# A decode attention kernel on one core: larger K/V chunks, an output summed in PSUM, and a last step of V that is multiplied turned

## The chip, the cores and the metric

The kernel runs on one core of a Trainium2 chip. The metric is device time in microseconds (us) of that core. "Before" is the kernel as it was, "after" is the changed kernel. A profile of one execution goes with every run; its span is about 2 us shorter than the time. All runs quoted here are of state fast. Times in the profiles are us from the start of the span. The engines are PE (TensorE), DVE (VectorE), ACT (ScalarE), POOL (GpSimd) and SP (SyncE, which here only issues DMAs).

## The reference

One token of 448 features attends to a cache of 65,536 positions, and the result is mixed with a small token MLP by a gate:

```python
B, Sq, D = 1, 1, 448
Hq, Hkv, Sk, Dh = 16, 8, 65536, 256
q = x @ wq                                 # 16 heads, two per K/V head
scores = einsum("bhqd,bhkd->bhqk", q, k) * Dh ** -0.5
o = einsum("bhqk,bhkd->bhqd", softmax(scores), v)
a = o.reshape(B, Sq, Hq * Dh) @ wo
b = ...                                    # layernorm, gelu MLP over F = 1792
g = sigmoid((x * gate_w).sum(-1, keepdims=True))
return g * a + (1 - g) * b                 # 448 numbers
```

All inputs are bf16. K and V together are 537 MB; they are read once. Everything else is small.

## The kernel before

A K/V head is cut in chunks, a chunk in steps of 16 blocks of 128 positions. K and V chunks take turns in a ring of four buffers. For every step, VectorE transposes K (L346), and TensorE multiplies it with the queries (L354). When a chunk's scores are complete, ScalarE takes the exponentials, VectorE transposes those, and TensorE multiplies them with V ("P.V", L376). At the end of a head, the sums are scaled, turned from rows into columns by an fp32 product, and projected with wo.

```python
SB = 16
SIZES = (4,) * 8          # steps per chunk: 4 steps are 32 KB per partition
RING = 4
# ... (cut)
    def load(item):       # items alternate: K of chunk i, V of chunk i
        last = sizes[-1]
        if item < 2 * total - 2:
            piece(item, 0, sizes[item // 2 % n_chunks] * SB)      # one DMA per chunk
        elif item == 2 * total - 1:                                # last chunk: 1 MB pieces
            for s in range(last - 1):
                piece(item - 1, s * SB, SB)                        # K 0, 1, 2
            piece(item, 0, SB)                                     # V 0
            piece(item - 1, (last - 1) * SB, SB)                   # K 3
            for s in range(1, last - 1):
                piece(item, s * SB, SB)                            # V 1, 2
            tail = SB // 2 - 2
            piece(item, (last - 1) * SB, SB - tail)
            piece(item, last * SB - tail, tail)
# ... (cut)
    for i in range(total):
        g, c = divmod(i, n_chunks)
        for s in range(sizes[c]):
            turn(i, s, n)          # VectorE: transpose K into kT[n % 2]
            scores(i, s, n)        # TensorE: 8 matmuls into sc[i % 2]
            # ... (cut: MLP, previous head's output)
        if 2 * i + RING < 2 * total:
            load(2 * i + RING)
        softmax(i)                 # ScalarE exp, VectorE transpose
        if c == n_chunks - 1:
            den_sum(g)
            den_tot(g)
        for s in range(sizes[c]):
            p_v(i, s)              # TensorE: 8 matmuls of 4 rows each (last step cut: in two parts)
        if 2 * i + 1 + RING < 2 * total:
            load(2 * i + 1 + RING)
        if c == n_chunks - 1:
            o_scale(g)             # VectorE: pvs = pv / denominator
    o_turn(HKV - 1)                # TensorE, fp32: rows to columns
    o_out(HKV - 1)                 # TensorE: @ wo; VectorE: + acc
    nc.sync.dma_start(out=out[0, 0].rearrange("(o n) -> o n", o=1), in_=res[:])
```

The softmax here doesn't subtract the row's maximum and nothing guards it: scores larger than these inputs give would overflow.

## Time and profile before

| | before |
|---|---|
| time, median of 3 | 1277.08 us (1277.07 to 1277.14) |
| span of the profile | 1275.1 us |
| busy: PE, DVE | 59%, 52% |
| DMA | 544.88 MB, 427 GB/s over the span |

The first fence is from the page: the busy share of the 16 DMA engines in 40 equal slices of the span, in tenths, and what they moved.

```profile
DMA  9999999999999999999999999999999999999996
GB/s 393 434 431 430 436 432 427 436 433 430 435 430 430 433 434 432 432 434 428 433 435 427 435 433 430 432 434 430 431 435 431 430 433 435 430 433 435 428 433 276
```

DMA is full from the second slice to the last but one. Only the beginning and the last slice (32 us) leave room, and in the last slice compute still has to finish what arrived last. The second fence is the timeline of before in that slice: start, duration, engine, line, operation, operands; in brackets the idle time of the engine before it and who ended it.

```profile
1239.05 2.31 DVE L346 STREAM_TRANSPOSE kT_183<-ring_70 128x2048 f32<-128x2048 f32 x1 [5.98 <-DMA ring_70<-in_A_k_cache_dram]
...
1257.28 2.27 DVE L346 STREAM_TRANSPOSE kT_183<-ring_72 128x2048 f32<-128x2048 f32 x1
1260.91 2.31 DVE L346 STREAM_TRANSPOSE kT_184<-ring_72 128x2048 f32<-128x2048 f32 x1 [1.36 <-DMA ring_72<-in_A_k_cache_dram]
1263.28 1.89 PE L354 MATMUL sc_75<-kT_184,qw 128*128 128x512 bf16 x8 [1.78 <-DVE kT_184 L346]
1265.21 0.60 ACT L361 ACTIVATE p_186<-sc_75 128x512 bf16<-128x512 f32 x1 [12.98 <-PE sc_75 L354]
...
1267.05 2.04 PE L376 MATMUL pv_77<-ring_73,pT_188 128*4 128x512 bf16 x32
...
1269.14 0.75 DVE L393 TENSOR_SCALAR pvs<-pv_77,rden 128x512 f32<-128x512 f32 x1 [1.61 <-PE pv_77 L376]
1269.94 1.05 PE L402 MATMUL misc<-sel,pvs 128*128 128x2 f32 x8 [0.85 <-DVE pvs L393]
...
1271.25 0.92 PE L412 MATMUL misc<-wo_97,oT 128*1 128x448 bf16 x4 [0.25 <-DVE oT L406]
1272.20 0.61 DVE L417 TENSOR_TENSOR res<-acc,misc 1x448 bf16<-1x448 f32 x1 [1.01 <-PE misc L412]
1272.84 0.32 SPq L452 DMA_DIRECT2D out_dram<-res  x1
```

Read it from the bottom. The store is issued at 1272.84. Before it stand, one after the other, the addition, the projection, the fp32 turn, the scaling and P.V. Further up, VectorE waited 1.36 us for the last piece of K (1260.91). What the timeline does not print is when the last piece of V landed. The trace's semaphore records give it: 1268.66, the last of the 16 increments that report this load (in what follows that time is its landing). The last weights load of P.V came at 1268.71, so the last K and the last V arrive at P.V together.

The trace's DMA records also give the time of single K/V packets (one row of a buffer is one packet):

```
before: packet bytes, count, median ns
 8192     896    309
32768   16128   1213
```

### The profile page before, as it was taken

The page shows a single profiled execution, that of the slowest core. Times are in us where ns is not written, and L with a number is a line of the kernel's source. Part 1 is how long each engine was busy: PE and PEld are TensorE (multiplying, and loading weights), DVE is VectorE, ACT ScalarE, POOL GpSimd, SP SyncE. Part 2 cuts the span into 40 slices and gives each one's busy share as a digit, 9 for nine tenths or more (in the row PEclk, how much of TensorE's full clock was granted, in tenths as well). Part 3 has the DMA queues.
Part 4 walks back from the last instruction along what each step waited for, and adds up shares of the span by engine and source line. Part 5 has one row for each costly group of instructions (what it writes and reads, how often), then busy time and mean ns, then how long its engine had stood idle before and what let it go on. Part 6 is the DMA issues. An engine that isn't in the chain of part 4 may idle for free.

```text
span 1275.1 us, 10091 instructions
## 1 busy us (share of the span) xinstructions
PE 758.4 (59%) x4374; PEld 288.1 (23%) x4374; DVE 661.7 (52%) x429; ACT 62.7 (5%) x159; POOL 83.1 (7%) x118
## 2 busy tenths in 40 slices
PE   3564656655566556656557565575655655656656
PEld 2121222212222222222122122221222222222212
DVE  7364455554464644646445455464453644545545
ACT  0000000000000000000000000000000000000000
POOL 3111012110021100210000000000000000000000
PEclk9888888888889887898888888788887888879789
DMA  9999999999999999999999999999999999999996
GB/s 393 434 431 430 436 432 427 436 433 430 435 430 430 433 434 432 432 434 428 433 435 427 435 433 430 432 434 430 431 435 431 430 433 435 430 433 435 428 433 276
DMA packets 21154, 544.88 MB, mean 427 GB/s; under 512 B 2675, under 2 KB 2806, under 8 KB 3958
## 3 DMA queue, kind: packets, MB, share of 16 engines
q1 hardware_dynamic: 19730, 540.55, 98.5%
q0 software_dynamic: 1376, 3.69, 0.8%
q8 instruction: 34, 0.56, 0.2%
q14 instruction: 10, 0.08, 0.0%
q10 hardware_dynamic: 4, 0.00, 0.0%
HBM read 544.22 MB, written 0.00 MB: 427 GB/s over the span
## 4 chain that ended last, share of the span: by engine, by line
DMA 64%; DVE 17%; PE 17%; issue 2%; DVEq 0%; SPq 0%; ACT 0%; ACTq 0%
DMA ring_70<-in_A_k_cache_dram 58%; PE sc_74 L354 14%; DVE kT_183 L346 9%; DVE kT_184 L346 7%; DMA ring_72<-in_A_k_cache_dram 6%; PE sc_75 L354 1%; PE misc L402 1%; DVE acc L337 1%; PE misc L412 1%; PE misc L325 0%; DVE acc L417 0%; PE pv_77 L376 0%; DVE pT_188 L365 0%; DVE oT L406 0%; DVEq L346 0%
## 5 line engine op out<-in xcount | busy, mean ns | idle before, releaser
L354 PEld LDWEIGHTS <-qw 128*128 128x128 bf16 x2048 | 222.3, 111 | 772.5 <-issue 324.5
L354 PE MATMUL sc_74<-kT_183,qw 128*128 128x512 bf16 x512 | 190.8, 536 | 239.6 <-DVE kT_183 L346 239.6
L346 DVE STREAM_TRANSPOSE kT_183<-ring_70 128x2048 f32<-128x2048 f32 x64 | 147.6, 2306 | 166.6 <-DMA ring_70<-in_A_k_cache_dram 146.7
L354 PE MATMUL sc_75<-kT_183,qw 128*128 128x512 bf16 x512 | 145.7, 433 | 114.7 <-DVE kT_183 L346 114.7
L346 DVE STREAM_TRANSPOSE kT_183<-ring_72 128x2048 f32<-128x2048 f32 x64 | 147.0, 2297 | 114.3 <-DMA ring_72<-in_A_k_cache_dram 91.7
L354 PE MATMUL sc_74<-kT_184,qw 128*128 128x512 bf16 x512 | 150.9, 445 | 25.4 <-DVE kT_184 L346 25.4
L346 DVE STREAM_TRANSPOSE kT_184<-ring_72 128x2048 f32<-128x2048 f32 x64 | 145.7, 2277 | 4.9 <-PE sc_75 L354 3.4
L346 DVE STREAM_TRANSPOSE kT_184<-ring_70 128x2048 f32<-128x2048 f32 x64 | 145.6, 2275 | 2.8 <-PE sc_74 L354 2.7
L354 PE MATMUL sc_75<-kT_184,qw 128*128 128x512 bf16 x512 | 131.7, 401 | 18.1 <-DVE kT_184 L346 18.1
L365 DVE STREAM_TRANSPOSE pT_187<-p_185 128x512 bf16<-128x512 bf16 x32 | 22.8, 712 | 103.4 <-ACT p_185 L361 103.4
L365 DVE STREAM_TRANSPOSE pT_188<-p_186 128x512 bf16<-128x512 bf16 x32 | 22.8, 712 | 86.7 <-ACT p_186 L361 86.7
L361 ACT ACTIVATE p_185<-sc_74 128x512 bf16<-128x512 f32 x32 | 19.1, 597 | 713.4 <-PE sc_74 L354 713.4
L376 PE MATMUL pv_77<-ring_71,pT_187 128*4 128x512 bf16 x512 | 30.4, 379 | 24.4 <-DVE pT_187 L365 24.4
L376 PE MATMUL pv_76<-ring_71,pT_187 128*4 128x512 bf16 x512 | 30.4, 379 | 24.4 <-DVE pT_187 L365 24.4
L376 PEld LDWEIGHTS <-pT_187 128*4 128x4 bf16 x1024 | 22.1, 86 | 87.3 <-DVE pT_187 L365 64.6
L376 PE MATMUL pv_77<-ring_73,pT_188 128*4 128x512 bf16 x512 | 30.6, 379 | 18.3 <-DVE pT_188 L365 18.3
L376 PE MATMUL pv_76<-ring_73,pT_188 128*4 128x512 bf16 x512 | 30.4, 379 | 18.3 <-DVE pT_188 L365 18.3
L361 ACT ACTIVATE p_186<-sc_75 128x512 bf16<-128x512 f32 x32 | 19.1, 597 | 449.5 <-PE sc_75 L354 449.5
L376 PEld LDWEIGHTS <-pT_188 128*4 128x4 bf16 x1024 | 22.1, 86 | 71.5 <-DVE pT_188 L365 48.4
L337 DVE SCALAR_TENSOR_TENSOR acc<-misc,half_g,acc 1x448 f32<-1x448 f32 x14 | 9.4, 672 | 53.1 <-PE misc L325 53.1
L314 POOL TENSOR_SCALAR t_b<-t_b 128x448 f32<-128x448 f32 x14 | 7.9, 567 | 361.3 <-ACT t_b L306 361.3
L139 POOL DMA_DIRECT2D wo_97<-in_A_wo_dram x4 | 3.1, 784 | 295.4 <-PE misc L412 295.4
(90 smaller groups left out, 201.9 us busy)
## 6 DMA issues: line engine op xcount, KB each, us to landing
ring_70<-in_A_k_cache_dram SPq DMA_DIRECT2D x32, 4096.0 KB, 26.5
ring_71<-in_A_v_cache_dram SPq DMA_DIRECT2D x32, 4096.0 KB, 29.8
ring_72<-in_A_k_cache_dram SPq DMA_DIRECT2D x31, 4096.0 KB, 29.4
ring_73<-in_A_v_cache_dram SPq DMA_DIRECT2D x31, 4096.0 KB, 33.9
ring_72<-in_A_k_cache_dram SPq DMA_DIRECT2D x4, 1024.0 KB, 27.5
ring_73<-in_A_wq_dram SPq DMA_DIRECT2D x1, 3072.0 KB, 10.4
ring_73<-in_A_v_cache_dram SPq DMA_DIRECT2D x3, 1024.0 KB, 26.9
wo_96<-in_A_wo_dram POOLq DMA_DIRECT2D x4, 448.0 KB, 15.1
```

What stands on the lines that cost most here:

```text
L139: nc.gpsimd.dma_start(out=wo_t[g % 2][:], in_=A_wo[g * 512:(g + 1) * 512, :].rearrange("(q p) n -> p q n", p=128),)
L314: nc.gpsimd.tensor_scalar(out=t_b[:], in0=t_b[:], scalar1=GELU_C1, scalar2=1.0, op0=ALU.mult, op1=ALU.add)
L337: nc.vector.scalar_tensor_tensor(out=acc[:], in0=misc[0:1, 0:D], scalar=half_g[0:1, 0:1], in1=acc[:], op0=ALU.mult, op1=ALU.add,)
L346: nc.vector.transpose(out=kT[n % 2][:].bitcast(FP32), in_=kn[:, s * SB * 128:(s + 1) * SB * 128])
L354: nc.tensor.matmul(sc[i % 2][:], lhsT=qw[:, g, q, PAD - s:PAD - s + 128], rhs=kv[:, :, q // 2, :, q % 2], start=(s == 0 and q == 0), stop= ...
L361: nc.scalar.activation(out=p_t[i % 2][:], in_=sc[i % 2][:], func=ACT.Exp, scale=scale, accum_out=den[g % 2][:, c:c + 1],)
L365: nc.vector.transpose(out=pT_t[i % 2][:], in_=p_t[i % 2][:])
L376: nc.tensor.matmul(pv[g % 2][32 * a:32 * a + 4, :], lhsT=pT[:, k, :, s], rhs=vt[:, j * DH:(j + 2) * DH], start=first and k < 4, stop=last ...
L402: nc.tensor.matmul(o_ps[:, 2 * c:2 * c + 2], lhsT=pvs[:, lo:lo + 128], rhs=sel[:, 2 * half:2 * half + 2], start=(half == 0), stop=(half == 1),
L412: nc.tensor.matmul(a_ps, lhsT=oT[:, 2 * c + r:2 * c + r + 1], rhs=wo_t[g % 2][:, 2 * r + c, :], start=(c == 0 and r == 0), stop=(c == 1 an ...
```

## The change

The change has three intents: fewer and larger packets (chunks of 5 or 4 steps, so 40 or 32 KB per partition), less work for VectorE (the output is summed in PSUM by TensorE, the queries are prepared one head at a time), and a shorter tail. For the tail, all pieces of the last K go ahead of V, and the last step of V is multiplied turned: V is the stationary operand, so its product comes out as columns and is added to the turned sum of the earlier steps, which can be turned before the last piece of V has landed. The core of the diff:

```diff
-SIZES = (4,) * 8
+SIZES = (5, 5, 5, 5, 4, 4, 4)
+TAIL = 4
 # load(), last chunk
-            for s in range(last - 1):
-                piece(item - 1, s * SB, SB)
-            piece(item, 0, SB)
-            piece(item - 1, (last - 1) * SB, SB)
-            for s in range(1, last - 1):
-                piece(item, s * SB, SB)
-            tail = SB // 2 - 2
-            piece(item, (last - 1) * SB, SB - tail)
-            piece(item, last * SB - tail, tail)
+            for s in range(last):
+                piece(item - 1, s * SB, SB)
+            for s in range(last - 1):
+                piece(item, s * SB, SB)
+            piece(item, (last - 1) * SB, SB - TAIL)
+            piece(item, last * SB - TAIL, TAIL)
 # ... (cut: denominators per chunk size, queries per head, MLP summed in PSUM)
+    def to_acc(col, rows, stop=False):          # 448 outputs as 4 groups of 112 columns
+        for a in range(4):
+            nc.tensor.matmul(acc[32 * a:32 * a + 1, 0:DQ], lhsT=col,
+                rhs=rows[:, DQ * a:DQ * (a + 1)], ..., tile_position=(0, 32 * a))
+    def p_v_turned(i, s, lo, hi):
+        for j in range(lo, hi):
+            for c in range(2):
+                at = (s * SB + j) * DH + c * 128
+                nc.tensor.matmul(o_ps[:, 2 * c:2 * c + 2], lhsT=vt[:, at:at + 128],
+                    rhs=pT[:, j, :, s], start=False, ...)
 # after the loop
-    o_turn(HKV - 1)
-    o_out(HKV - 1)
-    nc.sync.dma_start(out=out[0, 0].rearrange("(o n) -> o n", o=1), in_=res[:])
+    nc.vector.tensor_copy(out=pvs[:, 0:DH], in_=pv[g % 2][:, 0:DH])
+    nc.scalar.activation(out=pvs[:, DH:2 * DH], in_=pv[g % 2][:, DH:2 * DH], func=ACT.Copy)
+    o_turn(g)
+    p_v_turned(i, s, 0, SB - TAIL)
+    p_v_turned(i, s, SB - TAIL, SB)
+    nc.vector.tensor_tensor(out=oT..., in0=o_ps..., in1=rden..., op=ALU.mult)
+    o_out(g)
+    nc.vector.tensor_scalar(out=res[0:97, :], in0=acc[0:97, 0:DQ], scalar1=bias[0:97, 0:1], ...)
+    nc.sync.dma_start(out=out[0, 0].rearrange("(a n) -> a n", a=4), in_=res[0:97:32, :])
```

More of the change, by code (lines that the diff above doesn't have):

```diff
@@ L57 @@
     DR = D - DA
-    assert DR == 64 and F % 128 == 0 and SK % (128 * SB * sum(SIZES)) == 0
+    DQ = D // 4
+    assert DR == 64 and D % 4 == 0 and F % 128 == 0 and SK % (128 * SB * sum(SIZES)) == 0
     sizes = SIZES * (SK // (128 * SB * sum(SIZES)))
@@ L78 @@
     misc = psum.tile([128, 512], FP32, name="misc")
+    den_ps = psum.tile([128, 512], FP32, name="den_ps")
+    acc = psum.tile([128, 512], FP32, name="acc")
     total = HKV * n_chunks
@@ L132 @@
     nc.gpsimd.dma_start(out=w2T[:], in_=B_w2[:, 0].rearrange("(p b) -> p b", b=NF))
-    b2 = const.tile([1, 1], FP32)
-    nc.gpsimd.dma_start(out=b2[:], in_=B_b2.rearrange("(o n) -> o n", o=1))
+    zb = const.tile([1, 2], FP32)
+    nc.gpsimd.dma_start(out=zb[:, 1:2], in_=B_b2.rearrange("(o n) -> o n", o=1))
     wo_t = [const.tile([128, 4, D], BF16, name=f"wo{i}") for i in range(2)]
@@ L150 @@
     sel = const.tile([128, 4], FP32)
-    pick = const.tile([128, 2], FP32)
-    same = const.tile([128, 64, 2], FP32)
+    classes = sorted(set(sizes), reverse=True)
+    assert list(sizes) == sorted(sizes, reverse=True)
+    pick = const.tile([128, 2, len(classes)], FP32)
     nc.gpsimd.memset(sel[:], 0.0)
     nc.gpsimd.memset(pick[:], 0.0)
-    rows = [(sel, 4, -1, 32 * a) for a in range(4)]
-    rows += [(pick, 2, -16, 32 * a + s) for a in range(4) for s in range(MAXS)]
+    rows = [(sel[:], 4, -1, 32 * a) for a in range(4)]
+    for k, size in enumerate(classes):
+        rows += [(pick[:, :, k], 2, -16, 32 * a + s) for a in range(4) for s in range(size)]
     for t, w, step, row in rows:
         nc.gpsimd.affine_select(
-            out=t[:], in_=t[:], compare_op=ALU.not_equal, fill=1.0, base=-row,
+            out=t, in_=t, compare_op=ALU.not_equal, fill=1.0, base=-row,
             pattern=[[step, w]], channel_multiplier=1,
@@ L165 @@
         nc.gpsimd.memset(block[32 * a:32 * a + 32, a:a + 1], 1.0)
-    nc.gpsimd.tensor_copy(
-        out=same[:], in_=pick[:].rearrange("p (o r) -> p o r", o=1).to_broadcast([128, 64, 2])
-    )
     mhalf = const.tile([128, 1], FP32)
@@ L183 @@
     den = [work.tile([128, n_chunks], FP32, name=f"den{i}") for i in range(2)]
-    dsum = work.tile([128, 1], FP32, name="dsum")
-    rden = work.tile([128, 1], FP32, name="rden")
+    dsum = work.tile([128, len(classes)], FP32, name="dsum")
+    rden = work.tile([128, 2], FP32, name="rden")
     pvs = work.tile([128, 512], FP32, name="pvs")
     oT = work.tile([128, 4], BF16, name="oT")
-    acc = work.tile([1, D], FP32, name="acc")
-    half_g = work.tile([1, 1], FP32, name="half_g")
-    res = work.tile([1, D], BF16, name="res")
+    half_g = work.tile([128, 1], FP32, name="half_g")
+    bias = work.tile([128, 1], FP32, name="bias")
+    res = work.tile([128, DQ], BF16, name="res")
     qT = const.tile([128, 2, HQ], BF16)
-    qw = const.tile([128, HKV, 8, WIN], BF16)
+    qr = const.tile([128, 8, HQ], BF16)
+    qw = [const.tile([128, 8, WIN], BF16, name=f"qw{i}") for i in range(2)]
     gate = const.tile([128, 2], FP32)
-    nc.vector.memset(qw[:], 0.0)
-    for t in pv:
+    for t in pv + qw:
         nc.vector.memset(t[:], 0.0)
-    nc.vector.memset(acc[:], 0.0)
+    nc.vector.memset(acc[:, 0:DQ], 0.0)
     xd = const.tile([1, 2, 128], BF16)
@@ L221 @@
     nc.vector.tensor_tensor(out=xg, in0=x_row[:], in1=gw_row[:], op=ALU.mult)
-    z1 = const.tile([1, 1], FP32)
-    nc.vector.tensor_reduce(out=z1[:], in_=xg, axis=AXIS.X, op=ALU.add)
-    z_ps = misc[:, 500:501]
-    nc.tensor.matmul(z_ps, lhsT=one_f[:], rhs=z1[:], start=True, stop=True)
-    nc.scalar.activation(out=gate[:, 0:1], in_=z_ps, func=ACT.Exp, scale=-1.0)
-    nc.scalar.activation(out=gate[:, 1:2], in_=z_ps, func=ACT.Exp, scale=1.0)
+    nc.vector.tensor_reduce(out=zb[:, 0:1], in_=xg, axis=AXIS.X, op=ALU.add)
+    z_ps = misc[:, 500:502]
+    nc.tensor.matmul(z_ps, lhsT=one_f[:], rhs=zb[:], start=True, stop=True)
+    nc.scalar.activation(out=gate[:, 0:1], in_=z_ps[:, 0:1], func=ACT.Exp, scale=-1.0)
+    nc.scalar.activation(out=gate[:, 1:2], in_=z_ps[:, 0:1], func=ACT.Exp, scale=1.0)
     nc.vector.tensor_scalar(out=gate[:], in0=gate[:], scalar1=1.0, scalar2=None, op0=ALU.add)
     nc.vector.reciprocal(out=gate[:], in_=gate[:])
+    nc.vector.tensor_scalar(
+        out=half_g[:], in0=gate[:, 1:2], scalar1=0.5, scalar2=None, op0=ALU.mult
+    )
+    nc.vector.tensor_tensor(out=bias[:], in0=z_ps[:, 1:2], in1=gate[:, 1:2], op=ALU.mult)
     xb_ps = sc[0][:, 0:D]
@@ L281, with queries @@
             )
-    for g in range(HKV):
+    nc.vector.tensor_copy(out=qr[:].rearrange("p b h -> p (b h)"), in_=qr_ps)
+    def queries(g):
         for r in range(2):
@@ L286 @@
             nc.vector.tensor_tensor(
-                out=qw[:, g, :, cols],
-                in0=qr_ps.rearrange("p (b h) -> p b h", h=HQ)[:, :, h:h + 1].to_broadcast([128, 8, 4]),
+                out=qw[g % 2][:, :, cols], in0=qr[:, :, h:h + 1].to_broadcast([128, 8, 4]),
                 in1=block[:].rearrange("p (o a) -> p o a", o=1).to_broadcast([128, 8, 4]),
@@ L291 @@
             )
+    queries(0)
     load(RING - 1)
@@ L299 @@
     MIX = min(8, (n_steps - 4) // (NF + 1))
+    opened = set()
+    def to_acc(col, rows, stop=False):
+        for a in range(4):
+            nc.tensor.matmul(
+                acc[32 * a:32 * a + 1, 0:DQ], lhsT=col, rhs=rows[:, DQ * a:DQ * (a + 1)],
+                start=a not in opened, stop=stop, tile_position=(0, 32 * a),
+            )
+            opened.add(a)
     def mixer(n):
@@ L320, in mixer @@
             nc.gpsimd.tensor_scalar(
-                out=t_b[:], in0=t_b[:], scalar1=1.0, scalar2=None, op0=ALU.add
+                out=t_b[:], in0=t_b[:], scalar1=1.0, scalar2=half_g[:, 0:1], op0=ALU.add,
+                op1=ALU.mult,
             )
@@ L324, in mixer @@
         if ph == 5:
-            nc.tensor.matmul(
-                misc[0:1, 0:D], lhsT=w2T[:, b:b + 1], rhs=gel[:], start=True, stop=True
-            )
-            if b == 0:
-                nc.vector.tensor_scalar(
-                    out=half_g[:], in0=gate[0:1, 1:2], scalar1=0.5, scalar2=None, op0=ALU.mult
-                )
-                nc.vector.tensor_scalar(
-                    out=acc[:], in0=acc[:], scalar1=b2[0:1, 0:1], scalar2=gate[0:1, 1:2],
-                    op0=ALU.add, op1=ALU.mult,
-                )
-            nc.vector.scalar_tensor_tensor(
-                out=acc[:], in0=misc[0:1, 0:D], scalar=half_g[0:1, 0:1], in1=acc[:],
-                op0=ALU.mult, op1=ALU.add,
-            )
+            to_acc(w2T[:, b:b + 1], gel[:])
     def turn(i, s, n):
@@ L354, in scores @@
             nc.tensor.matmul(
-                sc[i % 2][:], lhsT=qw[:, g, q, PAD - s:PAD - s + 128], rhs=kv[:, :, q // 2, :, q % 2],
+                sc[i % 2][:], lhsT=qw[g % 2][:, q, PAD - s:PAD - s + 128], rhs=kv[:, :, q // 2, :, q % 2],
                 start=(s == 0 and q == 0), stop=(s == sizes[c] - 1 and q == 7),
@@ L365, in softmax, with p_v @@
         nc.vector.transpose(out=pT_t[i % 2][:], in_=p_t[i % 2][:])
-    def p_v(i, s, lo=0, hi=SB // 2):
+    def p_v(i, s):
         g, c = divmod(i, n_chunks)
@@ L371, in p_v @@
         first = c == 0 and s == 0
-        last = c == n_chunks - 1 and s == sizes[c] - 1
-        for k in range(lo, hi):
+        last = (g, c, s) == (HKV - 1, n_chunks - 1, sizes[c] - 2)
+        last |= g < HKV - 1 and c == n_chunks - 1 and s == sizes[c] - 1
+        for k in range(SB // 2):
             j = s * SB + 2 * k
@@ L381, in den_sum @@
     def den_sum(g):
-        nc.vector.tensor_reduce(out=dsum[:], in_=den[g % 2][:], axis=AXIS.X, op=ALU.add)
-    def den_tot(g):
-        d_ps = misc[:, 501:502]
-        nc.tensor.matmul(
-            d_ps, lhsT=same[:].rearrange("p o r -> p (o r)"), rhs=dsum[:], start=True, stop=True
-        )
-        nc.vector.reciprocal(out=rden[:], in_=d_ps)
-        nc.vector.tensor_tensor(out=rden[:], in0=rden[:], in1=gate[:, 0:1], op=ALU.mult)
-    def o_scale(g):
-        nc.vector.tensor_scalar(
-            out=pvs[:], in0=pv[g % 2][:], scalar1=rden[:, 0:1], scalar2=None, op0=ALU.mult
-        )
+        for k, size in enumerate(classes):
+            lo = sizes.index(size)
+            nc.vector.tensor_reduce(
+                out=dsum[:, k:k + 1], in_=den[g % 2][:, lo:lo + sizes.count(size)], axis=AXIS.X,
+                op=ALU.add,
+            )
+    def den_tot(g):
+        for k in range(len(classes)):
+            nc.tensor.matmul(
+                den_ps[:, 0:2], lhsT=dsum[:, k:k + 1].to_broadcast([128, 128]), rhs=pick[:, :, k],
+                start=(k == 0), stop=(k == len(classes) - 1),
+            )
+        nc.vector.reciprocal(out=rden[:], in_=den_ps[:, 0:2])
+        nc.vector.tensor_scalar(
+            out=rden[:], in0=rden[:], scalar1=gate[:, 0:1], scalar2=None, op0=ALU.mult
+        )
+    o_ps = misc[:, 504:508]
     def o_turn(g):
-        o_ps = misc[:, 504:508]
-        for c in range(2):
-            for half in range(2):
+        for half in range(2):
+            for c in range(2):
                 lo = half * DH + c * 128
@@ L403, in o_turn @@
                     o_ps[:, 2 * c:2 * c + 2], lhsT=pvs[:, lo:lo + 128], rhs=sel[:, 2 * half:2 * half + 2],
-                    start=(half == 0), stop=(half == 1),
+                    start=(half == 0 and c == 0), stop=(half == 1 and c == 1), skip_group_check=True,
                 )
-        nc.vector.tensor_copy(out=oT[:], in_=o_ps)
+    def p_v_turned(i, s, lo, hi):
+        vt = ring[(2 * i + 1) % RING]
+        pT = pT_t[i % 2][:].rearrange("p (j r x) -> p j r x", r=2, x=16)
+        for j in range(lo, hi):
+            for c in range(2):
+                at = (s * SB + j) * DH + c * 128
+                nc.tensor.matmul(
+                    o_ps[:, 2 * c:2 * c + 2], lhsT=vt[:, at:at + 128], rhs=pT[:, j, :, s],
+                    start=False, stop=(j == SB - 1 and c == 1), skip_group_check=True,
+                )
     def o_out(g):
-        a_ps = misc[0:1, 0:D]
         for c in range(2):
             for r in range(2):
-                nc.tensor.matmul(
-                    a_ps, lhsT=oT[:, 2 * c + r:2 * c + r + 1], rhs=wo_t[g % 2][:, 2 * r + c, :],
-                    start=(c == 0 and r == 0), stop=(c == 1 and r == 1),
-                )
-        dst = res if g == HKV - 1 else acc
-        nc.vector.tensor_tensor(out=dst[:], in0=acc[:], in1=a_ps, op=ALU.add)
+                to_acc(
+                    oT[:, 2 * c + r:2 * c + r + 1], wo_t[g % 2][:, 2 * r + c, :],
+                    stop=(g == HKV - 1 and c == 1 and r == 1),
+                )
         if g + 2 < HKV:
@@ L430 @@
                     o_turn(g - 1)
+                    for r in range(2):
+                        nc.scalar.activation(
+                            out=oT[:, r:4:2], in_=o_ps[:, r:4:2], func=ACT.Copy, scale=rden[:, r:r + 1]
+                        )
                 if s == 1:
@@ L439 @@
             den_tot(g)
-        for s in range(sizes[c]):
-            if i == total - 1 and s == sizes[c] - 1:
-                p_v(i, s, 0, SB // 4 + 1)
-                p_v(i, s, SB // 4 + 1)
-            else:
-                p_v(i, s)
+        for s in range(sizes[c] - (i == total - 1)):
+            p_v(i, s)
         if 2 * i + 1 + RING < 2 * total:
             load(2 * i + 1 + RING)
-        if c == n_chunks - 1:
-            o_scale(g)
-    o_turn(HKV - 1)
-    o_out(HKV - 1)
-    nc.sync.dma_start(out=out[0, 0].rearrange("(o n) -> o n", o=1), in_=res[:])
+        if c == n_chunks - 1 and g + 1 < HKV:
+            nc.scalar.activation(out=pvs[:], in_=pv[g % 2][:], func=ACT.Copy)
+            queries(g + 1)
+    g, i, s = HKV - 1, total - 1, sizes[-1] - 1
+    nc.vector.tensor_copy(out=pvs[:, 0:DH], in_=pv[g % 2][:, 0:DH])
[3 more added lines that the diff above has]
+    p_v_turned(i, s, SB - TAIL, SB)
+    nc.vector.tensor_tensor(
+        out=oT[:].rearrange("p (c r) -> p c r", r=2), in0=o_ps.rearrange("p (c r) -> p c r", r=2),
+        in1=rden[:].rearrange("p (o r) -> p o r", o=1).to_broadcast([128, 2, 2]), op=ALU.mult,
+    )
+    o_out(g)
+    nc.vector.tensor_scalar(
+        out=res[0:97, :], in0=acc[0:97, 0:DQ], scalar1=bias[0:97, 0:1], scalar2=None, op0=ALU.add
+    )
+    nc.sync.dma_start(
+        out=out[0, 0].rearrange("(a n) -> a n", a=4), in_=res[0:97:32, :]
+    )
 _INS = ['A_x', 'A_k_cache', 'A_v_cache', 'A_wq', 'A_wo', 'B_x', 'B_w1', 'B_b1', 'B_w2', 'B_b2', 'gate_w']
```

## The prediction

> **What bounds the kernel now.** DMA. By the slice view of the page, all 16 DMA engines are over 90% busy in every slice but the last, at 427 to 436 GB/s; the window view gives 432 GB/s from 40 to 1260 us. TensorE is busy 59%, VectorE 52%. The Trainium skill, "DMA: Bandwidth & Descriptors", section "Where 436 GB/s comes from", puts the fabric at 435.2 GB/s; the trace agrees (432), so at most 0.7% (9 us) is left in the rate for the same 544.9 MB. The chain of waits shows the K loads waiting behind other loads (26 to 34 us from issue to landing, with 9.7 us of transfer per 4 MB load): the queue always holds two to three chunks, so the buffers never starve it.
>
> **What the change does, costed.**
>
> 1. *Larger packets.* In the trace's DMA records a 32 KB packet took 1213 ns, an 8 KB one 309 ns: a line through both gives 7.7 ns fixed per packet and 27.18 bytes/ns. Chunks of 5 make packets of 40 KB: estimate 1514 ns. Each engine handles 896 K/V packets instead of 1024: 128 x 7.7 ns = about 1.0 us. On the critical path.
>
> 2. *Coarser ring.* K of chunk i+2 is requested once chunk i is transposed: 10.5 us after landing normally, 19 us at a head's end, while about 29 us of work is queued. With 5 steps both grow to about 14 and 22 us against 36. No starvation: 0 us.
>
> 3. *PSUM-summed output, denominators by class, queries per head, ACT eviction.* Removes the 9.4 us of one-partition accumulation (672 ns x 14), the 5 us memset of all queries and eight 0.75 us scalings from VectorE, adds small matmuls to TensorE. All hidden under DMA: 0 us. A few hundred more TensorE instructions mean one or two more 16 KB instruction fetches (0.6 us on one engine each): up to +0.6 us.
>
> 4. *Tail.* The only place where compute shows. Before (timeline from 1257 us): last K piece landed 1260.8; turn 2.3, scores 1.9, exp 0.6, transpose 0.7 us bring P.V to 1267.05; the last V piece's final semaphore increment is at 1268.66, and the last P.V weights load at 1268.71. So both paths meet. After that come scaling 0.75, output turn 1.07, cast 0.16, projection 0.93, sum 0.61, with gaps: store issued 1272.84, span end 1275.1. In the change all K pieces go before V, so the last K lands about 2.4 us sooner (one 1 MB piece); P.V of three steps, the copy (two halves on two engines, about 0.4 us) and the fp32 turn (about 1 us) overlap the last V landing. Behind the last V piece remain 8 turned matmuls (the q projection ran such pairs every 27 ns: 0.2 to 0.4 us), a 128x4 multiply (0.2), projection in four column groups (16 of 112 columns, about 0.45), and a 97x112 add (0.25). Estimate: store issued about 2.0 us after the last landing instead of 4.2.
>
> **Sum.** -1.0 (packets), +0.3 (fetches), -2.1 (tail): 1277.1 - 2.8 = about 1274.3 us. Range 1271.5 to 1277.0. Faster by over 2%: 1%; within 2%: 98%; slower by over 2%: 1%.
>
> **What would show it.** 1: 40 KB packets near 1514 ns, and mid-kernel rate 432.5 to 433 GB/s. 2: no slice of DMA below 9. 3: VectorE busy falls by about 15 us without a matching change of span. 4: last landing near 1267.9, store issue about 2 us later; last K transposed before 1259.
>
> **What would make it wrong.** A 40 KB row split into small packets (8 KB ones would cost 2% on those chunks, about +15 us); the slowest DMA engine (7.8 us behind the fastest at the last landing) drifting otherwise; the chain from the last K, not the last V, limiting the tail; four short output writes completing slower than one.

## The result, and the profile after

After took 1275.99 us (median of 4 runs, 1274.75 to 1276.86), before 1277.11 us in the same rounds (4 runs, 1277.07 to 1278.43). The ratio is 0.9988 with a 95% interval of 0.9971 to 1.0005. Ratios here are the mean time of one kernel's fast runs over that of the other's of the same rounds, so not quite the ratio of the medians. The time lies in the predicted range and within 2%, but the gain is 1.1 us where 2.8 were forecast, the interval includes no gain at all, and the runs of after lie 2 us apart.

The page after, same two lines as before:

```profile
DMA  9999999999999999999999999999999999999996
GB/s 400 423 436 430 433 433 435 435 428 433 435 430 434 429 436 432 434 430 431 436 432 429 438 428 433 433 433 434 429 437 431 432 432 429 439 430 435 428 430 271
```

DMA is full in the same slices. VectorE's busy time fell from 661.7 to 633.6 us, and none of it shows: both spans are 1275.1 us. The timeline of the tail after:

```profile
1252.98 8.85 DVE L351 STREAM_TRANSPOSE kT<-ring 128x2048 f32<-128x2048 f32 x4
...
1261.88 1.90 PE L359 MATMUL sc<-kT,qw 128*128 128x512 bf16 x8 [0.30 <-DVE kT L351]
...
1263.81 0.60 ACT L366 ACTIVATE p<-sc 128x512 bf16<-128x512 f32 x1 [11.51 <-PE sc L359]
...
1265.88 1.96 PE L382 MATMUL pv<-ring,pT 128*4 128x512 bf16 x24
...
1267.87 0.42 DVE L472 COPY pvs<-pv 128x256 f32<-128x256 f32 x1 [1.46 <-PE pv L382]
1268.33 0.38 ACT L473 ACTIVATE pvs<-pv 128x256 f32<-128x256 f32 x1 [3.83 <-DVE pvs L472]
1268.35 1.86 PE L414 MATMUL misc<-sel,pvs 128*128 128x2 f32 x8 [0.52 <-DVE pvs L472]
1270.08 0.99 PE L425 MATMUL misc<-pT,ring 128*128 128x2 bf16 x32
1271.11 0.16 DVE L477 TENSOR_TENSOR oT<-misc,rden 128x4 bf16<-128x4 f32 x1 [2.81 <-PE misc L425]
1271.33 0.54 PE L314 MATMUL acc<-wo,oT 128*1 128x112 bf16 x16 [0.25 <-DVE oT L477]
1271.92 0.33 DVE L482 TENSOR_SCALAR res<-acc,bias 97x112 bf16<-97x112 f32 x1 [0.65 <-PE acc L314]
1272.28 0.65 SPq L485 DMA_DIRECT2D out_dram<-res  x1
```

Four things stand out against before.

- The last V landed at 1267.87 (semaphore records), 0.79 us sooner. The larger packets do what was said: a 40 KB packet took 1514 ns at the median of 8,192, exactly the estimate.
- The store was issued 4.41 us after that landing, not 2.0. Copy, fp32 turn and all 32 turned pairs came after the last V had landed; they were meant to be over before, but for 8 pairs (a pair is a weights load and its matmul).
- VectorE ran the last chunk's four transposes back to back (8.85 us from 1252.98) and waited for no K. The last K had landed at 1258.06, 2.7 us sooner than in before (1260.79), but its transpose starts at 1259.56 only.
- The fp32 turn took 1.86 us where it took 1.05 in before. P.V of three steps took 1.96 us where four took 2.04.

The last point is TensorE's clock. The window view shows the granted clock (PEclk), which the trace records as either 1.00 or 0.50. The rows of after:

```profile
1246.00:1266.00 20.00, 15.11 (x94) 6.17 (x95) 13.71 (x11) 1.38 (x4) 0.00 (x0) 0.99 0.87 367
1266.00:1271.00 5.00, 4.48 (x64) 3.07 (x56) 0.81 (x3) 0.38 (x1) 0.00 (x0) 0.57 0.06 24
```

(Columns: window, us, then busy us of PE, PEld, DVE, ACT, POOL, then PEclk, DMA share, GB/s.) From 1266.72 on TensorE ran at half clock. The same stretch in before and in after:

```profile
1266.72:1270.13 3.41, 2.54 (x36) 1.26 (x36) 1.08 (x3) 0.00 (x0) 0.00 (x0) 1.00 0.06 24
1266.72:1270.13 3.41, 2.89 (x22) 1.93 (x15) 0.42 (x1) 0.38 (x1) 0.00 (x0) 0.50 0.03 13
```

In before the clock fell only at 1272.69, when TensorE was done. The Trainium skill, "TensorE: Matmul & The Clock Gate", section "Part 1: The HAM clock gate", says that the clock has these two states, set by TensorE's recent activity in windows of 3413 ns which run freely and do not restart with the kernel. The trace agrees: the changes of the granted clock lie whole multiples of 3.41 us apart (1246.24 to 1266.72 is six). So where they fall against the tail can change from run to run.

Finally, the store itself got slower. A row of 448 numbers took 0.32 us to issue and 1.12 us from issue to landing (1272.84 to 1273.96); four rows of 112 took 0.65 and 1.65 us (1272.28 to 1273.94). This eats 0.53 us of the 0.56 by which the store is issued sooner, and explains why the two profiled spans are equal. The semaphore records place the loss at the beginning: the first increment came 0.44 us after the issue with one row and 1.03 us with four, and from the first to the last it took 0.68 and 0.63 us.

### The profile page after: what moved, and what is told of

Same layout as the page of the kernel before. It is cut to its first block, busy times and chain, and to the rows that moved or that the text cites. A ratio compares the mean times of both kernels' runs of the same rounds, so it can differ in the third digit from the quotient of the medians.

```text
span 1275.1 us, 10452 instructions
## 1 busy us (share of the span) xinstructions
PE 729.7 (57%) x4552; PEld 285.1 (22%) x4552; DVE 633.6 (50%) x396; ACT 64.3 (5%) x165; POOL 76.9 (6%) x137
## 4 chain that ended last, share of the span: by engine, by line
DMA 72%; PE 12%; DVE 11%; issue 5%; POOL 0%; DVEq 0%; ACT 0%; POOLq 0%
DMA ring<-in_A_k_cache_dram 70%; PE sc L359 11%; DVE kT L351 11%; DMA zb<-in_B_b_dram 2%; PE misc L414 0%; PE pv L382 0%; DVEq L351 0%; PE acc L314 0%; ACT p L366 0%; PE misc L425 0%; DVE pT L370 0%; DVE qw L294 0%; DVE h_bc L257 0%; POOL w1T L132 0%; PE den_ps L398 0%
## 5 line engine op out<-in xcount | busy, mean ns | idle before, releaser
L359 PE MATMUL sc<-kT,qw 128*128 128x512 bf16 x2048 | 587.3, 442 | 431.5 <-DVE kT L351 430.7
L351 DVE STREAM_TRANSPOSE kT<-ring 128x2048 f32<-128x2048 f32 x256 | 577.3, 2292 | 454.7 <-DMA ring<-in_A_k_cache_dram 367.5
L382 PE MATMUL pv<-ring,pT 128*4 128x512 bf16 x2040 | 120.4, 380 | 73.4 <-DVE pT L370 73.4
L370 DVE STREAM_TRANSPOSE pT<-p 128x512 bf16<-128x512 bf16 x56 | 39.8, 711 | 152.6 <-ACT p L366 152.6
L366 ACT ACTIVATE p<-sc 128x512 bf16<-128x512 f32 x56 | 33.4, 597 | 1052.0 <-PE sc L359 1052.0
L382 PEld LDWEIGHTS <-pT 128*4 128x4 bf16 x2040 | 44.7, 87 | 142.8 <-DVE pT L370 95.7
L336 POOL TENSOR_TENSOR t_b<-t_b,u_b 128x448 f32<-128x448 f32 x14 | 16.0, 1140 | 1.2
L343 POOL TENSOR_TENSOR gel<-t_b,u_b 128x448 bf16<-128x448 f32 x14 | 15.8, 1130 | 1.2
L414 PEld LDWEIGHTS misc<-sel,pvs 128*128 128x128 f32 x64 | 10.7, 238 | 3.5 <-issue 1.5
L366 ACT ACTIVATION_READ_ACCUMULATOR p<-sc 128x1 f32 x56 | 10.9, 194 | 0.0
```

Of the source, the lines that this page charges most:

```text
L336: nc.gpsimd.tensor_tensor(out=t_b[:], in0=t_b[:], in1=u_b[:], op=ALU.mult)
L343: nc.gpsimd.tensor_tensor(out=gel[:], in0=t_b[:], in1=u_b[:], op=ALU.mult)
L351: nc.vector.transpose(out=kT[n % 2][:].bitcast(FP32), in_=kn[:, s * SB * 128:(s + 1) * SB * 128])
L359: nc.tensor.matmul(sc[i % 2][:], lhsT=qw[g % 2][:, q, PAD - s:PAD - s + 128], rhs=kv[:, :, q // 2, :, q % 2], start=(s == 0 and q == 0), s ...
L366: nc.scalar.activation(out=p_t[i % 2][:], in_=sc[i % 2][:], func=ACT.Exp, scale=scale, accum_out=den[g % 2][:, c:c + 1],)
L370: nc.vector.transpose(out=pT_t[i % 2][:], in_=p_t[i % 2][:])
```

## The experiments

Two theories were set against each other at first. Theory V is the prediction's: the last V landing sets the end. Theory K: the end is set by the chain through the last K, whose pace also depends on TensorE's clock. Twelve kernels were run in four calls, each beside before (median 1277.16, 1277.11, 1277.15 and 1277.06 us in the four calls). All gave correct results. The table lists, for each profile, the start of the last transpose of K, the last V landing, the mean spacing of the passes of the fp32 turn (115 ns is full clock, 216 half), and the issue of the store.

| run | last K transpose | last V landed | fp32 pass, ns | store issued (after landing) | median, us (range) | ratio to before |
|---|---|---|---|---|---|---|
| before | 1260.91 | 1268.66 | 115 | 1272.84 (4.18) | | |
| after | 1259.56 | 1267.87 | 216 | 1272.28 (4.41) | 1275.99 (1274.75 to 1276.86) | 0.9988 |
| after_again | 1260.05 | 1267.94 | 217 | 1272.32 (4.37) | 1276.55 (1274.74 to 1277.39) | 0.9994 |
| no_turned | 1258.97 | 1267.88 | 115 | 1270.91 (3.04) | 1276.54 (1275.43 to 1277.19) | 0.9993 |
| warm | 1259.88 | 1267.97 | 115 | 1271.12 (3.15) | 1275.22 (1275.08 to 1276.13) | 0.9986 |
| chunks4 | 1260.44 | 1268.55 | 115 | 1271.47 (2.91) | 1275.52 (1275.25 to 1276.04) | 0.9988 |
| before_k_first | 1259.89 | 1269.27 | 115 | 1273.55 (4.28) | 1277.79 (1277.05 to 1278.86) | 1.0004 |
| k_early | 1260.45 | 1268.16 | 115 | 1273.59 (5.42) | 1279.18 (1278.08 to 1279.49) | 1.0011 |
| k_early_turn2 | 1260.32 | 1267.77 | 115 | 1273.91 (6.14) | 1278.68 (1278.47 to 1279.88) | 1.0011 |
| k_early_store2 | 1260.39 | 1267.74 | 115 | 1273.94 (6.20) | 1278.79 (1278.59 to 1279.25) | 1.0011 |
| prev_pieces | 1259.19 | 1268.23 | 216 | 1271.45 (3.22) | 1275.52 (1274.64 to 1276.13) | 0.9987 |
| prev_no_turned | 1258.54 | 1268.26 | 216 | 1272.49 (4.23) | 1276.07 (1275.34 to 1276.87) | 0.9990 |
| prev_warm | 1259.17 | 1267.98 | 115 | 1270.42 (2.43) | 1274.33 (1273.97 to 1274.82) | 0.9978 |
| prev_warm_chunks4 | 1259.28 | 1269.00 | 115 | 1270.65 (1.65) | 1275.03 (1274.65 to 1275.38) | 0.9983 |

### after_again: the changed kernel once more

> The changed kernel unaltered, so that the other runs have a neighbour of the same chip. Theory K (the tail is set by the chain that starts at the last K and ends in the fp32 turn, and TensorE runs it at full or half clock as it falls): about 1276 us with a spread of 1 us or more over the rounds, last landing near 1267.9, and the store issued 3.5 to 4.5 us after it. Theory V (the prediction's: the last V landing sets the end): store issued 2 us after the landing, spread as small as that of before (0.1 us).

It was 1276.55 us, with 2.65 us between its fastest and slowest round; the nine runs of before of that call lie 1.07 us apart. The store came 4.37 us after the landing. Theory V's 2 us after the landing are out. That the landing moved by only 0.07 us between the profiles of after and after_again says nothing of the spread, since these two executions took the same time (1276.86 and 1276.88 us). The next run has the same landing (1267.88) in an execution 1.38 us shorter. The spread of before was larger than expected, too.

### no_turned: without the turned last step

```diff
-        for s in range(sizes[c] - (i == total - 1)):
+        for s in range(sizes[c]):
             p_v(i, s)
 # ... (cut: which matmul closes the sum)
-    p_v_turned(i, s, 0, SB - TAIL)
-    p_v_turned(i, s, SB - TAIL, SB)
```

> Only the turned last step is undone: all four steps of the last chunk go through the ordinary P.V, then the two half copies and the fp32 turn. Theory K: the same as the changed kernel or up to 0.5 us faster, because 32 turned pairs (0.87 us) are replaced by 8 ordinary matmuls (0.43 us) on the chain that sets the end. Theory V: 1.5 to 2 us slower, because copy (0.45) and fp32 turn (1.05 to 1.86) now stand behind the last V landing.

1276.54 us against 1276.55 of after_again: no gain from the turned step, the centre of the change, is seen as the kernel stands. The rounds of both scatter (standard deviations 1.0 and 0.8 us), so that the difference of the means, 0.02 us, has a 95% interval of about 1.3 us to either side: theory V's 1.5 to 2 us are excluded, a few tenths are not. Its profile caught full clock and an early chain (last transpose at 1258.97), and there P.V did wait for V, half a microsecond:

```profile
1265.29 1.47 PE L382 MATMUL pv<-ring,pT 128*4 128x512 bf16 x24
1267.30 1.00 PE L382 MATMUL pv<-ring,pT 128*4 128x512 bf16 x8 [0.54 <-DMA ring<-in_A_v_cache_dram]
1268.82 1.05 PE L414 MATMUL misc<-sel,pvs 128*128 128x2 f32 x8 [0.52 <-DVE pvs L472]
```

So the two chains end close together, and which one is last can differ between executions. Two profiles of different clock are not to be compared; the medians are.

### warm: TensorE is kept busy in the tail

```diff
+    def warm(k):       # a product that nothing reads
+        for _ in range(k):
+            nc.tensor.matmul(warm_ps[:], lhsT=qw[(HKV - 1) % 2][:, 0, 0:128],
+                rhs=kT[(n_steps - 1) % 2][:, 0:512], start=True, stop=True)
         softmax(i)
+        if i == total - 1:
+            warm(6)
 # after the loop, ahead of the copies
+    warm(2)
```

> Eight matmuls of 128x512 whose product nobody reads fill the two gaps of TensorE in the tail (six while the last exponentials and their transpose run, two during the copy). Same result. If the half clock at the end is what lengthened the tail: the granted clock stays at full to the end, the passes of the fp32 turn come every 112 ns instead of 213, and the median falls by 0.5 to 1.2 us with a spread under 0.5 us. If the clock does not matter: no change, or up to 0.4 us slower from the added work.

The added matmuls ran in the gaps, and the clock stayed up to 1270.75, as the second window shows:

```profile
1246.00:1266.00 20.00, 16.33 (x94) 6.57 (x94) 13.76 (x10) 1.38 (x4) 0.00 (x0) 0.98 0.88 368
1266.00:1271.00 5.00, 4.45 (x85) 2.78 (x84) 1.22 (x5) 0.39 (x1) 0.00 (x0) 0.98 0.06 23
```

The median fell by 1.33 us to 1275.22, with 1.05 us between fastest and slowest round (less was expected: under 0.5). In the profiles, copy to store took 3.39 us (1267.73 to 1271.12) against 4.42 in after_again (1267.90 to 1272.32). That is 1.03 us for the same instructions, and so what the half clock costs where it falls in the tail. The medians alone would not prove it, since the fastest round of after_again (1274.74) beats every round of warm; prev_pieces and prev_warm below show it again. Of the changed kernel and its variants, leaving out the early-K runs, the three profiles with the added matmuls kept full clock past 1270; of the six without them four fell to half clock between 1265.99 and 1267.69, and two (no_turned, chunks4) did not.

### chunks4: packets of 32 KB again

```diff
-SIZES = (5, 5, 5, 5, 4, 4, 4)
+SIZES = (4,) * 8
```

> Only the chunk sizes are undone: eight chunks of 4 steps, packets of 32 KB. If the gain of the larger packets reaches the end (7.7 ns per packet, 128 packets per engine): last landing and time 0.8 to 1.0 us later than in the changed kernel. If the packets gave nothing, or something else hides their gain: last landing within 0.3 us, time the same.

Its last landing was 0.61 us after that of after_again, a little under the 0.8 to 1.0 expected; its time was 1.0 us shorter, not longer. Its profile shows full clock in the tail, where that of after_again shows half, so this pair cannot tell the packets from the clock. The comparison was made again below, with unread matmuls on both sides.

### before_k_first: the order of the pieces alone, in the kernel before

```diff
-            for s in range(last - 1):
+            for s in range(last):
                 piece(item - 1, s * SB, SB)
-            piece(item, 0, SB)
-            piece(item - 1, (last - 1) * SB, SB)
-            for s in range(1, last - 1):
+            for s in range(last - 1):
                 piece(item, s * SB, SB)
```

> The kernel before with one part of the change alone: all four K pieces of the last chunk ahead of its V. In before the last P.V weights load (1268.71) came 0.05 us after the last V landing (1268.66), so if V set its end: last landing unchanged near 1268.6, store issued at 1272.8 as before, time within 0.3 us. If the last K set its end: about 1.2 us faster.

1277.79 us over 4 runs (ratio 1.0004, interval 0.9989 to 1.0019): no gain. P.V started 1.06 us sooner than in before (1265.99), and then waited for V, first 0.91 and then 0.34 us:

```profile
1265.99 1.49 PE L374 MATMUL pv<-ring,pT 128*4 128x512 bf16 x24
...
1268.38 0.59 PE L374 MATMUL pv<-ring,pT 128*4 128x512 bf16 x5 [0.91 <-DMA ring<-in_A_v_cache_dram]
1269.31 0.39 PE L374 MATMUL pv<-ring,pT 128*4 128x512 bf16 x3 [0.34 <-DMA ring<-in_A_v_cache_dram]
```

In before, then, no gain from the order of K alone is seen, since V is as late. (The last landing was 0.6 us later here than in the profile of before, with the same packets. With one profile of each it stays open whether that is chance or the new order.)

### k_early, k_early_turn2, k_early_store2: the last K ten microseconds sooner

```diff
 # ... (cut: the V of the chunk before is left out of its usual place, in load() and in the main loop)
             for s in range(last):
                 piece(item - 1, s * SB, SB)
+            piece(item - 2, 0, last * SB)          # V of the chunk before, now behind the last K
 # main loop: P.V of the chunk before waits until the last scores are done
+        if i == total - 1:
+            for s in range(sizes[c]):
+                p_v(i - 1, s)
```

k_early_turn2 also turns the last two steps of V; k_early_store2 splits the four-row store of that in two stores of two rows, on two queues.

> The changed kernel with the last chunk's K loaded ahead of the V of the chunk before it, and that chunk's P.V moved behind the last scores, so that the last K lands 10 us sooner. Same bytes, same result. Theory K: the last transpose of K falls before 1257 us instead of 1259.6 to 1260.4, P.V waits for V and not for K, and the store is issued at 1269.9 (full clock) to 1271 (half clock) instead of 1272.3; time 1274 to 1275. Theory V: the end does not move, since the last V landing stays at 1267.9.

> As k_early, with the last two steps turned instead of one, so that copies and the fp32 turn are over before the third V piece lands. Then only turned pairs, the multiply and the projection stand behind the last landing. Theory K: store issued 1.7 to 2.2 us after the last landing (which is what the prediction had said of the change), 1269.6 to 1270.1; time 1273.8 to 1274.6, nearly without spread since the fp32 turn is off the path whatever the clock. If k_early is not slower than this, the fp32 turn was not on the path.

> As k_early_turn2, with the four-row store split in two stores of two rows on the queues of SyncE and ScalarE. The four-row store took 0.65 us to issue and 1.66 us from issue to landing, the one-row store of before 0.32 and 1.12. If the cost goes with rows per issue: about 0.45 us each, end 0.2 to 0.3 us sooner than k_early_turn2. If it is in the short writes themselves: no change.

All three missed. Their medians were 1.6 to 2.1 us above that of before (the intervals of the ratio, 0.9998 or 0.9999 to 1.0024, just reach 1), and the last transpose of K came at 1260.32 to 1260.45, not before 1257. TensorE in k_early:

```profile
1249.33 1.90 PE L361 MATMUL sc<-kT,qw 128*128 128x512 bf16 x8 [0.29 <-DVE kT L353]
1254.95 5.33 PE L361 MATMUL sc<-kT,qw 128*128 128x512 bf16 x16 [3.72 <-DVE kT L353]
1260.58 1.90 PE L361 MATMUL sc<-kT,qw 128*128 128x512 bf16 x8 [0.31 <-DVE kT L353]
1262.77 1.90 PE L361 MATMUL sc<-kT,qw 128*128 128x512 bf16 x8 [0.29 <-DVE kT L353]
...
1266.77 3.20 PE L384 MATMUL pv<-ring,pT 128*4 128x512 bf16 x56
```

None of these waits is for a DMA. TensorE waits for VectorE, VectorE for the exponentials of the chunk before (a gap of 3.72 us on TensorE), 16 matmuls took 5.33 us because the clock was at half from 1255.37 to 1258.78, after that gap, and P.V of 32 more matmuls stands after the last scores. The edit itself put these into the tail (3.20 us of P.V where no_turned's 24 matmuls took 1.47), so the longer time says nothing on theory K; the last transpose, late without a wait for a DMA, does. So the form of theory K in which the landing of the last K sets the end falls as well. What remains is theory B, a backlog: from the landing of the K of the chunk before the last, VectorE and TensorE have no slack up to the store. In after that chunk's first transpose waited 5.78 us for its whole 4 MB and started at 1238.77, 33.5 us ahead of the store:

```profile
1238.77 4.50 DVE L351 STREAM_TRANSPOSE kT<-ring 128x2048 f32<-128x2048 f32 x2 [5.78 <-DMA ring<-in_A_k_cache_dram]
```

Splitting the store did not help: from the store's issue to its landing took 1.84 us against 1.65.

### prev_pieces: the K of the chunk before the last in four pieces

```diff
     def load(item):
         last = sizes[-1]
-        if item < 2 * total - 2:
+        if item == 2 * total - 4:
+            for s in range(last):
+                piece(item, s * SB, SB)
+        elif item < 2 * total - 2:
```

> The changed kernel with the K load of the chunk before the last cut into four 1 MB loads, nothing else. The early-K runs showed that the last K's landing does not set the end. Theory B (backlog: from the landing of the chunk before's whole K, at 1238.8, VectorE and TensorE work without a wait to the store, 33.5 us): VectorE starts on that chunk about 6 us sooner, the last K is transposed when it lands (near 1258.1 instead of 1259.6 to 1260.4), store issued at 1269.6 to 1271 instead of 1272.3, time 1274 to 1275. Rival L (the chain after the last K takes as long whatever stands before it, because the last V or the clock sets it): store issued within 0.4 us of 1272.3 where the clock is at half, 1271.1 where it is full.

VectorE now did that chunk's transposes from 1233.46 on, in one row without a wait, and was idle 5.42 us ahead of the last chunk's K. The backlog was gone:

```profile
1233.46 8.85 DVE L354 STREAM_TRANSPOSE kT<-ring 128x2048 f32<-128x2048 f32 x4
...
1248.63 3.59 PE L385 MATMUL pv<-ring,pT 128*4 128x512 bf16 x32 [4.37 <-DMA ring<-in_A_v_cache_dram]
1251.15 2.31 DVE L354 STREAM_TRANSPOSE kT<-ring 128x2048 f32<-128x2048 f32 x1 [5.42 <-DMA ring<-in_A_k_cache_dram]
1253.52 5.13 PE L362 MATMUL sc<-kT,qw 128*128 128x512 bf16 x16 [1.30 <-DVE kT L354]
```

The store was issued at 1271.45 at half clock, 0.87 us sooner than in after_again at half clock, and the median was 1275.52 us (after_again: 1276.55, with ranges that overlap). So theory B holds in the profiles, and rival L, which allowed 0.4 us, does not; the times bear it out at full clock, in prev_warm below. It was worth less than hoped: TensorE, now idle 4.37 us, was at half clock from 1246.35 to 1256.59 (16 matmuls in 5.13 us), and the last transpose came at 1259.19 and not at 1258.1. The time missed the expected 1274 to 1275 by half a microsecond.

### prev_no_turned: the turned step, where V is late enough

```diff
 # prev_pieces, with the edit of no_turned
```

> As prev_pieces, without the turned last step. Theory B: with the backlog gone the last V landing is what the tail waits for, so that now the turned step is worth what the prediction gave it: this run is 0.7 to 1.5 us slower than prev_pieces, its store issued about 3.0 us after the last landing. If the turned step is worth nothing even then: the same time.

P.V waited for V again, and both profiles have the tail at half clock, so they may be compared: the store was issued at 1272.49, 1.04 us after that of prev_pieces.

```profile
1267.67 1.23 PE L385 MATMUL pv<-ring,pT 128*4 128x512 bf16 x8 [0.86 <-DMA ring<-in_A_v_cache_dram]
1269.42 1.86 PE L417 MATMUL misc<-sel,pvs 128*128 128x2 f32 x8 [0.52 <-DVE pvs L475]
```

In the medians the turned step was worth 0.55 us (1276.07 against 1275.52), with ranges that overlap. So by these profiles it pays when the last V is what the tail waits for; in the change as it was made no gain was seen.

### prev_warm: both cures together

```diff
 # prev_pieces, with the edit of warm
```

> As prev_pieces, with the eight unread matmuls of the run warm. Clock theory: full clock to the store, store issued at 1269.5 to 1270.2, time 1273.5 to 1274.3, spread under 1 us; the best version. If prev_pieces already runs its tail at full clock: the same as prev_pieces within 0.3 us.

1274.33 us (1273.97 to 1274.82), ratio 0.9978 with an interval of 0.9965 to 0.9990: the fastest version. (The intervals of prev_pieces, 0.9974 to 0.9999, and of prev_warm_chunks4, 0.9970 to 0.9997, also lie under 1.) Against warm, which differs by the load in pieces alone, it is 0.89 us faster in the median, and the ranges do not overlap (warm: 1275.08 to 1276.13); its store is issued 0.70 us sooner, at full clock in both. The chips differ, but before took 1277.16 and 1277.15 us. This is the cleanest evidence for theory B. Against prev_pieces, the unread matmuls gave 1.19 us. Its tail:

```profile
1263.24 1.45 PE L371 MATMUL warm_ps<-kT,qw 128*128 128x512 bf16 x6
...
1265.50 1.47 PE L394 MATMUL pv<-ring,pT 128*4 128x512 bf16 x24
...
1267.50 1.05 PE L426 MATMUL misc<-sel,pvs 128*128 128x2 f32 x8
1268.42 0.97 PE L437 MATMUL misc<-pT,ring 128*128 128x2 bf16 x32
...
1270.42 0.66 SPq L500 DMA_DIRECT2D out_dram<-res  x1
```

The store is issued 1.86 us sooner than in after; the fp32 turn takes 1.05 us again. It even began before the last V landed (1267.98), as the prediction had it, but the turned pairs started 0.44 us after the landing, behind that turn. The expected 1273.5 to 1274.3 was missed by a hair: 16 matmuls of the last chunk still ran at half clock, after the wait for V at 1248.

### prev_warm_chunks4: the packets, with the clock held

```diff
 # prev_warm, with the edit of chunks4
```

> As prev_warm, with eight chunks of 4 steps (32 KB packets). In the run chunks4 the last landing was 0.6 to 0.7 us later than with 40 KB packets, but its time was not longer than the changed kernel's, whose clock differs from round to round. Here both sides run their tail at full clock. If the gain of the packets reaches the end: last landing near 1268.6, store issued near 1271.0, time 0.5 to 0.9 us over prev_warm's 1274.33. If it does not reach the end: within 0.3 us of 1274.33.

The last landing was 1.02 us later than in prev_warm, and the median 0.70 us longer (1275.03 against 1274.33). In the two profiles the store was only 0.23 us later, because there the last V landed while the turned pairs were running (1268.65 to 1269.62) and the store followed 1.65 us behind it. So the larger packets seem to reach the end, with 0.2 us in the profiles and 0.7 in the medians. This is less sure than the landing: the ranges overlap a little, the two runs are of different chips, and not all else was held. With chunks of one size the denominators take 0.38 us of TensorE instead of 0.61, and in the last chunk prev_warm ran 16 matmuls at half clock that prev_warm_chunks4 ran at full; both favour the small packets, so that their loss may be larger than seen.

Over all profiles, the last landing was at 1268.87 on average with 32 KB packets (before, before_k_first, chunks4, prev_warm_chunks4) and at 1267.98 with 40 KB packets (the other ten): 0.89 us for a predicted 1.0. (These kernels differ in more than their packets; the two pairs that differ in the chunk sizes alone give 0.61 and 1.02.)

## Why the prediction was right or wrong

The time fell in the range, and the call "within 2%" was right. The range reached to 0.1 us below the time of before, so that almost any gain would have hit it; that is no proof of the mechanism. Of the forecast gain of 2.8 us, 1.1 came. Point by point, by the prediction's own steps:

1. *"Larger packets ... about 1.0 us. On the critical path."* The mechanism and its size were right: 1514 ns per packet, last landing 0.6 to 1.0 us sooner. (The rate of the middle, forecast at 432.5 to 433 GB/s, is 432 before and after in the window view from 40 to 1260 us; so small a gain does not show in it.) "On the critical path" was right only in part: 0.2 to 0.7 us seem to reach the end where unread matmuls hold the clock in the tail; in the change itself the difference is lost in what the clock does.
2. *"Coarser ring ... 0 us."* Right: no slice of DMA fell below 9.
3. *"All hidden under DMA: 0 us."* Right, though the size was off: VectorE lost 28.1 us of work, not 15, and the span did not move. Of the extra instruction fetches, forecast at one or two of 16 KB and up to 0.6 us, one came (35 packets of that size where before has 34); such packets took 0.95 to 0.96 us at the median, and what the extra one cost at the end was not measured.
4. *"P.V of three steps, the copy ... and the fp32 turn (about 1 us) overlap the last V landing ... store issued about 2.0 us after the last landing instead of 4.2."* This is the step that failed. The store came 4.41 us after the landing. Three things stood in its place. First, the prediction took the K chain's lead from the landing of the last K ("the last K lands about 2.4 us sooner"). That landing did come 2.7 us sooner, but VectorE had waited for it only 1.36 us in before, and the chain behind it was already full from the K of the chunk before. Cutting that one load in pieces made the store 0.87 us sooner at half clock and 0.70 at full. Second, TensorE fell to half clock in the tail; keeping it busy gave 1.33 us in the median of after_again and 1.19 in that of prev_pieces. The prediction read all durations of the tail from a profile in which the clock happened to be full. Third, four short output rows cost 0.53 us more than one; the prediction named this as a risk and put no number on it.

With the first two taken away (prev_warm), the time is 2.8 us below before, which is the sum the prediction had named for the change as it stood. That the sums agree is partly chance, since prev_warm still pays the slower store and its store is issued 2.43 us after the landing.

What stays open: which activity keeps TensorE's clock up. The busy time of the profile does not decide it. In after the window from 1263.31 to 1266.72 had 1.85 us of TensorE work in it and was followed by half clock; in chunks4 the window from 1264.48 to 1267.89 had 1.84 us and was not; in warm the one from 1267.34 to 1270.75 had 3.11 us and was. Also open is why four short rows take longer to issue and to land; the split over two queues shows only that fewer rows per store are no cure. And one thing was not tried: in before the 16 increments of the last V load came between 1260.85 and 1268.66, 1264.7 on average. If all had come together, the last would have come about 4.0 us sooner (an estimate from these 16 times), more than the change had hoped for.

## What to carry to other kernels

In this kernel, bound by DMA, the tail behind the last bytes is what a change of compute could win, and it had to be followed back further than the last load: look for the last point where the compute engines were idle (here the K of the chunk before the last), and cut that load in pieces first. Do not read the tail's durations from one profile: check the granted clock there, and where TensorE has gaps like those filled here (1.6 and 0.5 us), filling them with matmuls that nothing reads can be worth as much as the change under study. Compare small changes of the tail only with the same clock on both sides.

## What the Trainium skill lacked or had wrong

- "TensorE: Matmul & The Clock Gate" tells of two clock states, of idle gaps longer than a window, and of short idles between groups of matmuls that also make the clock fall. It does not say what counts as a busy window: one with 1.85 of 3.41 us busy in the profile was followed by half clock, one with 1.84 was not, and one with 3.11 was.
- "DMA: Bandwidth & Descriptors" has no durations for large packets of a stream. Here they were 309, 1213 and 1514 ns for 8, 32 and 40 KB, or 7.7 ns per packet and 27.18 bytes per ns on each engine.
- The same page has a least round trip for tiny transfers and a row size below which they are slower, but not what a store of a few short rows costs: one row of 896 bytes took 0.32 us to issue and 1.12 to land, four rows of 224 bytes took 0.65 and 1.65.
- No page was found that tells how far the 16 DMA engines drift apart over one kernel (the DMA page says of two of them that they are usually slower, without a figure): in before the 16 semaphore increments of the last V load came from 1260.85 to 1268.66, and those of a load that landed at 83.8 us lay 1.9 us apart.
